# A fused channel attention and gated MLP on one core: x's product issued in the last step of the block before, its moves two steps earlier

## The chip, the cores and the metric

The kernel runs on one core of a Trainium2 chip. The metric is the device time of one execution, in microseconds (us). Each kernel is timed in several runs and the median counts; one more execution is recorded by the hardware profiler, and all rows below come from that one.

The engines are called PE (matrix products), PEld (its weight loads), DVE (vector), ACT (scalar and activation), POOL (GpSimd) and SP (here it only issues transfers). Each engine works through its own queue in program order; engines wait for each other by semaphores. A name such as L582 is line 582 of the kernel before.

## The reference

Two batches of q, k and v, each 6016 x 256, float32. In each batch the columns of q and k are normalised over the 6016 rows, a 256 x 256 score matrix is formed and its softmax `a` taken; then comes x = v a, followed by RMS normalisation of each row and a gated MLP with 1536 hidden channels:

```python
qn = q / (np.linalg.norm(q, axis=1, keepdims=True) + 1e-06)
kn = k / (np.linalg.norm(k, axis=1, keepdims=True) + 1e-06)
s = kn.transpose(0, 2, 1) @ qn / tau
...
a = np.exp(s)
a /= a.sum(-1, keepdims=True) + 1e-09
x = v @ a
...
rms = np.sqrt(np.mean(x * x, axis=-1, keepdims=True) + 1e-06)
xn = x / rms * rms_g
g = xn @ w_gate
silu = g * (1.0 / (1.0 + np.exp(-g)))
val = xn @ w_val
out = silu * val @ w_out
```

## The kernel before

**Stages.** The kernel first reads q and k of batch 0 in chunks and forms the scores, the norms and the softmax. From then on it goes through 24 blocks j of 512 rows (128 x 4; blocks 11 and 23 have three tiles of 128), 12 of each batch. Each block has 12 steps f, one for 128 hidden channels. Blocks 0 and 1 use the plain product (`emit_hidden`) beside the rest of batch 1's scores and the decoding of the weights; blocks 2 to 23 use `emit_pair`, which makes gate and value of a step from seven half-size products (a Strassen-Winograd scheme).

**Precision.** All products are made of pairs: each operand is split into a high part (`vh`, `gh`, `xt0`, `w100`) and the remainder (`vl`, `gl`, `xt1`, `w101`), and three matmuls stand for one product. ACT writes the high part (a copy into a rounded type) and POOL or DVE subtracts it to get the remainder.

**One step of `emit_pair`.** PE makes 21 matmuls `p` (L582) in four groups of 3, 6, 6 and 6, each into a PSUM tile of its own. The pool of these tiles (`ps_gv`) has four, so group g of a step must wait until group g of the step before has been read. ACT copies the first group to `a` (L595), DVE adds up the rest in L601 (needs `a` and the second group), L602 and L603 (third group) and L604 (fourth group), which leaves gate and value in `z`. In the odd step of a pair ACT applies Silu (L600) and POOL multiplies (L612, twice); in the even step behind it ACT rounds the product to `gh` (L553, twice) and POOL makes `gl` (L559, twice). Three steps later PE adds the step's part of the output, 12 matmuls `po` (L662). In step 2 the output of the block before is complete: ACT copies it to `ob` (L673) and SP issues four stores (L680).

**The next block's input.** While block j runs, the input of block n = j + 1 is made, in pieces that a table `ready` hangs behind the steps of block j (the pieces of one step follow that step's `emit_pair` and `emit_out` in every engine's queue):

- `x(h)`: half h of x = v a, 12 matmuls `px` (L386) on PE from `vt`, the split v, and `a`.
- `squares_of_x(h)`: ACT squares it and sums each row (L402); POOL makes 1/rms `rr` (L411, L415).
- `xn(h)`: ACT scales x by `rr` into `xn` (L427).
- `emit_xT_move`: DVE transposes 32 x 32 squares of `xn` into `xw` (L463, twice), and SP issues 16 transfers from `xw` to `xnT` (L470), which move the squares to their places.
- `v_moves`: DVE transposes the v of the block after next into `vw` (L366, twice), then SP issues four loads for the v one further on (L335). `v_splits`: ACT and POOL split it into `vt` (L349, L350).
- `emit_xT_parts`: ACT waits for all 16 transfers and scales `xnT` by the RMS weight (L485, twice); DVE makes the four differences of the Winograd scheme (L490, then L495 twice).
- `emit_xT_round(0)`, `emit_xT_round(1)`: ACT rounds (L507) and POOL subtracts (L509), two each, into `xt`, which the p products of the next block read.

Block 1 shares this table with the later ones; block 0 has its own, `ready0`. In blocks 4 to 7 and 10 the pieces of batch 1's softmax are added in steps 6 to 8 (`inverse_norms`, `softmax_min`, `softmax_exp`, `softmax_div`).

Of the kernel before, what the change touches and what calls it, by code (L numbers as in the profile page):

```python
# [19 lines left out]
def kernel(  # L20
# [59 lines left out]
    def f32(ap):  # L80
        return ap.bitcast(F32)
# [24 lines left out]
    def decode_w(f, piece=None):  # L106
        if piece in (None, 0):
            r = wraw[f]
            x = pool["wtmp"].tile([P, WF], U32, tag="wx", name=f"wx_{f}")
            nc.vector.tensor_scalar(  # L110
                out=x, in0=r[:, :, 0], scalar1=29, scalar2=None, op0=ALU.logical_shift_right
            )
            wval[f] = x
        if piece in (None, 1):
            x = wval[f]
            high = wraw.pop(f)[:, :, 1]
            e = pool["wtmp"].tile([P, WF], F32, tag="we", name=f"we_{f}", bufs=1)
            nc.scalar.activation(out=e, in_=high.bitcast(F32), func=AF.Copy, scale=2.0 ** -112)
            nc.vector.scalar_tensor_tensor(
                out=x, in0=high, scalar=0x80000000, in1=x,  # L120
                op0=ALU.bitwise_and, op1=ALU.bitwise_or,
            )
            wval[f] = (x, e)
        if piece in (None, 2):
            x, e = wval[f]
            nc.vector.scalar_tensor_tensor(
                out=x, in0=e.bitcast(U32), scalar=3, in1=x,
                op0=ALU.logical_shift_left, op1=ALU.bitwise_or,
            )
            wval[f] = x.bitcast(F32)  # L130
# [187 lines left out]
    for b in range(B):  # L318
        t = 0
        while t < NT:  # L320
            n = min(BT, NT - t)
            blocks.append((b, t * A, n))
            t += n
    NB = len(blocks)
# [4 lines left out]
    def load_v(j, queue=nc.sync):  # L329

        b, mu0, n = blocks[j]
        t = v_p.tile([P, A * BT, KC, S], F32, tag="v", name=f"v_{j}")
        src = v[b].rearrange("(s m) (c i r) -> i s m c r", s=S, c=KC, i=A)
        for i in range(A):
            queue.dma_start(  # L335
                out=t[S * i:S * (i + 1), :A * n].rearrange("p m c r -> p (m c) r"),
                in_=src[i][:, mu0:mu0 + A * n].rearrange("s m c r -> s (m c) r"),
            )
        v_t[j] = t

    def half_tiles(j, h):
        return list(range(2 * h, min(2 * h + 2, blocks[j][2])))
# [17 lines left out]
    def move_v(j, c):  # L360

        n = blocks[j][2]
        if c == 0:
            v_w[j] = v_p.tile([P, KC, BN], F32, tag="vw", name=f"vw_{j}")
        w = v_w[j][:, c]
        nc.vector.transpose(  # L366
            out=by_tile(w, n),
            in_=v_t[j][:, :A * n, c, :].rearrange("p (a t) r -> p a t r", a=A),
        )

    def split_v(j, c, engine=nc.vector):
        n = blocks[j][2] * P
        if c == 0:
            vT[j] = [vt_p.tile([P, KC, BN], F32R, tag=f"vt{i}", name=f"vt{i}_{j}") for i in range(2)]
        split(v_w[j][:, c, :n], [x[:, c, :n] for x in vT[j]], engine)

    def emit_x(j, h):
        ah, al = a_hl[blocks[j][0]]
        vh, vl = vT[j]
        ts = half_tiles(j, h)  # L380
        psum, tag = (ps_s, "s") if j >= WINO and h else (ps_m, "m") if j else (ps_gv, "gv")
        px = psum.tile([P, 2, C], F32, tag=tag, name=f"px_{j}_{h}")
        for c in range(KC):
            for i, t in enumerate(ts):
                for m, (w, x) in enumerate(((vh, ah), (vl, ah), (vh, al))):
                    nc.tensor.matmul(  # L386
                        out=px[:, i, :], lhsT=w[:, c, t * P:(t + 1) * P], rhs=x[:, c, :],
                        start=(i == 0 and c == 0 and m == 0),
                        stop=(c == KC - 1 and m == 2),
                        skip_group_check=True,  # L390
                    )
        xps[j, h] = px

    def emit_x_squares(j, h):
        px = xps[j, h]
        ts = half_tiles(j, h)
        if h == 0:
            xnt[j] = xn_p.tile([P, BT, C], F32, tag="xn", name=f"xn_{j}")
        xn = xnt[j][:, 2 * h:2 * h + 2, :]
        ss = st_p.tile([P, 2], F32, tag="ss", name=f"ss_{j}_{h}")  # L400
        for i in range(len(ts)):
            nc.scalar.activation(  # L402
                out=xn[:, i, :], in_=px[:, i, :], func=AF.Square, scale=C ** -0.5,
                accum_out=ss[:, i:i + 1],
            )
        xps[j, h] = (px, ss)

    def emit_rr(j, h):
        px, ss = xps[j, h]
        nn = len(half_tiles(j, h))  # L410
        nc.gpsimd.tensor_scalar(  # L411
            out=ss[:, :nn], in0=ss[:, :nn], scalar1=1e-6, scalar2=None, op0=ALU.add
        )
        rr = st_p.tile([P, 2], F32, tag="rr", name=f"rr_{j}_{h}")
        nc.gpsimd.tensor_tensor(out=rr[:, :nn], in0=ss[:, :nn], in1=mhalf[:, :nn], op=ALU.pow)  # L415
        xps[j, h] = (px, rr)

    def emit_xn(j, h, share=False):
        px, rr = xps.pop((j, h))
        for i, t in enumerate(half_tiles(j, h)):  # L420
            if share and i == 0:
                nc.vector.tensor_scalar(
                    out=xnt[j][:, t, :], in0=px[:, i, :], scalar1=rr[:, i:i + 1], scalar2=None,
                    op0=ALU.mult,
                )
                continue
            nc.scalar.activation(  # L427
                out=xnt[j][:, t, :], in_=px[:, i, :], func=AF.Copy, scale=rr[:, i:i + 1]
            )
# [67 lines left out]
    def emit_xT_round(j, i):  # L497
        h = blocks[j][2] * P // 2
        slots = ((0, 1), (1, 3)) if i == 0 else ((3, 5), (5, 7))
        hi, lo = ([y[:, a:b] for a, b in slots] for y in xp[j])  # L500
        if i == 0:
            x = [moved[j][0][:, c, :2 * h].rearrange("p (i n) -> p i n", i=2) for c in range(KC)]
            src = [x[0][:, :1], x[1]]
        else:
            src = [moved[j][1][:, m:m + 2, :h] for m in (0, 2)]
        for o, x in zip(hi, src):
            nc.scalar.activation(out=o, in_=x, func=AF.Copy)  # L507
        for o, x, y in zip(lo, src, hi):
            nc.gpsimd.tensor_tensor(out=o, in0=x, in1=f32(y), op=ALU.subtract)  # L509
# [174 lines left out]
    with tc.manual_schedule():  # L684
# [40 lines left out]
        for i in range(nch):  # L725
            n = chunks[0][i][1]
# [84 lines left out]
        for f in range(NF):  # L811
            go = [lambda: None]
            if f + 3 < NF:
                go = [lambda f=f: decode_w(f + 3, 0), lambda f=f: decode_w(f + 3, 1)]
# [7 lines left out]
            n = 2 if f % 2 else 1  # L822
# [44 lines left out]
        def v_moves(n):  # L867
            if n < NB:
                move_v(n, 0)
                move_v(n, 1)  # L870
                if 2 < n + 1 < NB:
                    load_v(n + 1)

        def v_splits(n):
            if n < NB:
                for c in range(KC):
                    split_v(n, c, nc.gpsimd)

        def x(h):
            return lambda n: emit_x(n, h)  # L880

        def squares_of_x(h):
            return lambda n: (emit_x_squares(n, h), emit_rr(n, h))

        def xn(h):
            return lambda n: emit_xn(n, h)

        ready = {
            0: (x(0),),
            2: (squares_of_x(0), x(1)),  # L890
            3: (xn(0),),
            4: (squares_of_x(1), lambda n: v_moves(n + 1)),
            5: (xn(1), emit_xT_move),
            6: (lambda n: v_splits(n + 1),),
            7: (emit_xT_parts,),
            8: (lambda n: emit_xT_round(n, 0),),
            10: (lambda n: emit_xT_round(n, 1),),
        }
        ready0 = {
            1: (v_moves,),  # L900
# [10 lines left out]
        for s, (j, f) in enumerate(steps):  # L911
            if j < WINO:
                emit_hidden(j, f, weights.get((j, f), ()))
            else:
                emit_pair(j, f)
            owed.append((j, f))
            if len(owed) > (2 if j < WINO else 3):
                emit_out(*owed.pop(0))
            n = j + 1
            if n < NB:  # L920
                for go in (ready if j else ready0).get(f, ()):
                    go(n)
            for go in extra.get((j, f), []):
                go()
# [37 lines left out]
```

## Time and profile before

| | us |
|---|---|
| runs of the kernel before (three) | 1510.26, 1510.35, 1511.95 |
| median | 1510.35 |
| the profiled execution | 1509.38 |
| its span, first to last instruction | 1507.6 |
| PE busy in the span | 1356.1 |
| POOL busy | 949.9 |
| DVE busy | 931.0 |
| ACT busy | 679.7 |
| mean granted clock of PE | 0.937 of full speed |

The profiled execution took 1.8 us more than its span. Busy PE is counted from start to modelled end of pipelined matmuls. A wait is idle time of an engine just before an instruction, put down to what released that instruction last. The granted clock of a stretch is 1.00 at full speed (2.4 GHz) and 0.50 at the lower level (1.2 GHz).

### The profile page before, as it was taken

The numbers are of one execution on the slowest core, as the hardware profiler recorded it, in microseconds if no ns is written. First come the engines' busy times: TensorE is split into PE (matmuls) and PEld (weight loads), VectorE is DVE, ScalarE is ACT, GpSimd is POOL, SyncE is SP. The second block draws the span as 40 slices with busy tenths as digits, with TensorE's granted clock in tenths as the row PEclk, the third lists the DMA queues.
The fourth block names the chain that finished last, engine by engine and source line by source line (L and its number), as shares of the span: only waits on it lengthen the run. The fifth ranks groups of instructions, "written<-read, shape, count | busy, mean of one in ns | idle before, by whom it ended". The sixth has DMA issues, their size and how long they took to land.

```text
span 1507.6 us, 27090 instructions
## 1 busy us (share of the span) xinstructions
PE 1356.1 (90%) x10212; PEld 1312.5 (87%) x10212; DVE 931.0 (62%) x1417; ACT 679.7 (45%) x1331; POOL 949.9 (63%) x824
## 2 busy tenths in 40 slices
PE   7998988899898898898898898898998988988988
PEld 6877878889898898898898898898998988988988
DVE  5689567556755665665664665665566556656655
ACT  4556545444444454443443443444444444444433
POOL 3146556766766676676765767666667766766664
PEclk8999999999998899999998999999999999999999
DMA  8857210120120110110110210201201201101001
GB/s 258 293 168 210 50 28 15 29 43 15 29 43 15 30 35 10 39 30 14 39 29 15 39 25 19 43 15 29 43 15 29 42 17 29 34 9 27 21 7 24
DMA packets 147683, 71.77 MB, mean 48 GB/s; under 512 B 100704, under 2 KB 139104, under 8 KB 147552
## 3 DMA queue, kind: packets, MB, share of 16 engines
q1 hardware_dynamic: 147168, 68.99, 18.3%
q0 software_dynamic: 384, 1.05, 0.4%
q8 instruction: 81, 1.33, 0.4%
q14 instruction: 50, 0.41, 0.1%
HBM read 46.40 MB, written 12.32 MB: 39 GB/s over the span
## 4 chain that ended last, share of the span: by engine, by line
PE 56%; DVE 14%; SPq 14%; issue 5%; DMA 5%; ACT 2%; POOL 2%; DVEq 0%; ACTq 0%; POOLq 0%
PE p L582 30%; PE po L662 16%; SPq L470 14%; PE px L386 4%; PE s L174 3%; DVE z L601 3%; DMA xnT<-xw 3%; DMA raw<-in_k_dram 2%; DVE z L602 2%; DVE z L604 2%; POOL z L612 2%; DVE vw L366 1%; ACT xnT L485 1%; DVE z L603 1%; PE pg L630 1%
## 5 line engine op out<-in xcount | busy, mean ns | idle before, releaser
L582 PE MATMUL p<-xt,w 128*128 128x256 f32 (+1 forms) x3168 | 494.6, 292 | 118.4 <-ACT a L595 80.1
L582 PEld LDWEIGHTS p<-xt,w 128*128 128x128 f32 x3168 | 436.1, 198 | 127.7 <-ACT a L595 85.1
L612 POOL TENSOR_TENSOR z<-z,z 128x512 f32<-128x512 f32 (+1 forms) x262 | 326.1, 1265 | 297.2 <-DVE z L604 297.2
L559 POOL TENSOR_TENSOR gl<-z,gh 128x512 fp32r<-128x512 f32 (+1 forms) x272 | 346.5, 1294 | 122.1 <-ACT gh L553 121.3
L662 PE MATMUL po<-w,gh 128*128 128x256 f32 x2256 | 417.0, 283 | 0.2 <-ACT gh L553 0.2
L662 PEld LDWEIGHTS po<-w,gh 128*128 128x128 f32 x2256 | 354.0, 193 | 2.4 <-ACT gh L553 0.4
L601 DVE TENSOR_TENSOR z<-p,a 128x512 f32<-128x512 f32 (+1 forms) x264 | 178.8, 677 | 282.2 <-PE p L582 270.9
L582 PE MATMUL p<-xt,s 128*128 128x256 f32 (+1 forms) x2376 | 344.1, 292 | 6.5 <-POOL xt L509 3.1
L582 PEld LDWEIGHTS p<-xt,s 128*128 128x128 f32 x2376 | 317.9, 200 | 8.1 <-DVE z L601 4.0
L662 PE MATMUL po<-w,gl 128*128 128x256 f32 x1128 | 317.8, 282 | 2.6 <-POOL gl L559 2.4
L595 ACT ACTIVATE a<-p 128x256 f32<-128x256 f32 (+1 forms) x264 | 99.1, 375 | 333.8 <-PE p L582 333.5
L553 ACT ACTIVATE gh<-z 128x512 fp32r<-128x512 f32 (+1 forms) x274 | 167.9, 621 | 133.8 <-POOL z L612 120.9
L662 PEld LDWEIGHTS po<-w,gl 128*128 128x128 f32 x1128 | 215.5, 191 | 3.4 <-POOL gl L559 3.2
L602 DVE TENSOR_TENSOR z<-p,z 128x512 f32<-128x512 f32 (+1 forms) x264 | 179.4, 680 | 33.1 <-PE p L582 7.1
L604 DVE TENSOR_TENSOR z<-p,z 128x512 f32<-128x512 f32 (+1 forms) x264 | 179.4, 680 | 28.8 <-PE po L662 0.5
L600 ACT ACTIVATE z<-z 128x1024 f32<-128x1024 f32 (+1 forms) x132 | 136.4, 1034 | 63.8 <-DVE z L604 63.7
L603 DVE TENSOR_TENSOR z<-p,z 128x256 f32<-128x256 f32 (+1 forms) x264 | 110.4, 418 | 9.0
L490 DVE TENSOR_TENSOR xp<-xnT 128x512 f32<-128x512 f32 (+1 forms) x22 | 15.3, 695 | 149.2 <-ACT xnT L485 149.2
L174 PE MATMUL s<-raw 128*128 128x256 f32 x376 | 94.4, 409 | 13.4 <-DMA raw<-in_k_dram 13.3
L485 ACT ACTIVATE xnT<-xnT,g_sb 128x512 f32<-128x512 f32 (+1 forms) x44 | 28.9, 703 | 169.7 <-DMA xnT<-xw 169.7
L174 PEld LDWEIGHTS s<-raw 128*128 128x128 f32 x376 | 75.8, 206 | 28.0 <-issue 16.6
L198 DVE TENSOR_TENSOR acc<-acc,sq 128x1024 f32<-128x1024 f32 (+1 forms) x47 | 64.0, 1362 | 31.1 <-ACT sq L189 28.9
(91 smaller groups left out, 1112.4 us busy)
## 6 DMA issues: line engine op xcount, KB each, us to landing
out_dram<-ob SPq DMA_DIRECT2D x88, 128.0 KB, 2.3
raw<-in_q_dram SPq DMA_DIRECT2D x20, 512.0 KB, 6.0
raw<-in_k_dram SPq DMA_DIRECT2D x20, 512.0 KB, 6.9
v<-in_v_dram SPq DMA_DIRECT2D x80, 128.0 KB, 3.7
xnT<-xw SPq DMA_DIRECT2D x320, 32.0 KB, 1.9
wraw<-in_moe_w_gate_dram SPq DMA_DIRECT2D x12, 256.0 KB, 3.8
wraw<-in_moe_w_val_dram SPq DMA_DIRECT2D x12, 256.0 KB, 3.9
wraw<-in_moe_w_out_dram SPq DMA_DIRECT2D x12, 256.0 KB, 5.0
```

The costliest lines, as they stand in the source:

```text
L174: nc.tensor.matmul(out=s_ps[b][:, c, :], lhsT=r[:, 1, t, c * P:(c + 1) * P], rhs=r[:, 0, t, :], start=(t0 + t == 0 and c == 0), stop=(t0 + ...
L470: nc.sync.dma_start(out=x[S * i:S * (i + 1), :, a * n * S:(a + 1) * n * S], in_=w[S * a:S * (a + 1), :, i, :n, :].rearrange("p c t s -> p ...
L553: nc.scalar.activation(out=gh, in_=hh, func=AF.Copy)
L559: engine.tensor_tensor(out=gl, in0=hh, in1=f32(gh), op=ALU.subtract)
L582: nc.tensor.matmul(out=t[:, i, :h], lhsT=wm[wi], rhs=xm[xi], start=(i == 0 and q == 0), stop=(q == 2), skip_group_check=True,)
L600: nc.scalar.activation(out=zg[:, :2 * n], in_=zg[:, :2 * n], func=AF.Silu)
L601: nc.vector.tensor_tensor(out=zz[:, 0:4:3], in0=ps[1], in1=twice(a1[:, :, :h]), op=ALU.add)
L602: nc.vector.tensor_tensor(out=zz[:, 1:3], in0=ps[2], in1=twice(zz[:, 3:4]), op=ALU.add)
L603: nc.vector.tensor_tensor(out=zz[:, 3], in0=ps[2][:, 0], in1=zz[:, 2], op=ALU.add)
L604: nc.vector.tensor_tensor(out=zz[:, 1:3], in0=ps[3], in1=zz[:, 1:3], op=ALU.add)
L612: engine.tensor_tensor(out=hh, in0=hh, in1=z[:, i * n:(i + 1) * n], op=ALU.mult)
L662: nc.tensor.matmul(out=o_ps[j][t // 2][:, t % 2, :], lhsT=g[:, t * P:(t + 1) * P], rhs=wo[w][:, f, :], start=(first and t % 2 == 0 and m = ...
```

## The change

The table `ready` becomes three. Blocks 2 to 22 use the new `ready`, block 1 gets `ready1`, block 0 keeps `ready0`. In the new `ready`:

- the first half of x's product, for block j + 2, is issued in step 11 of block j (it was in step 0 of block j + 1), the second half in step 0 (was step 2);
- squares, `rr` and `xn` of both halves stand two steps earlier: steps 0 to 3 instead of 2 to 5;
- the transposes and the 16 transfers (`emit_xT_move`) stand in step 3 instead of step 5, which is ahead of `v_moves` (still in step 4) instead of behind it;
- scaling and differences (`emit_xT_parts`) stay in step 7, the rounds in steps 8 and 10.

`ready1` has the moves in step 4, `v_moves` in step 5, the scaling in step 8 and the rounds in steps 9 and 10, and issues the first half of block 3's product in step 11. No instruction is added or taken away in these pieces.

```diff
         ready = {
-            0: (x(0),),
-            2: (squares_of_x(0), x(1)),
-            3: (xn(0),),
-            4: (squares_of_x(1), lambda n: v_moves(n + 1)),
-            5: (xn(1), emit_xT_move),
+            0: (squares_of_x(0), x(1)),
+            1: (xn(0),),
+            2: (squares_of_x(1),),
+            3: (xn(1), emit_xT_move),
+            4: (lambda n: v_moves(n + 1),),
             6: (lambda n: v_splits(n + 1),),
             7: (emit_xT_parts,),
             8: (lambda n: emit_xT_round(n, 0),),
             10: (lambda n: emit_xT_round(n, 1),),
+            11: (lambda n: n + 1 < NB and emit_x(n + 1, 0),),
+        }
+        ready1 = {
+            0: (x(0),),
+            1: (squares_of_x(0),),
+            2: (x(1), xn(0)),
+            3: (squares_of_x(1),),
+            4: (xn(1), emit_xT_move),
+            5: (lambda n: v_moves(n + 1),),
+            6: (lambda n: v_splits(n + 1),),
+            8: (emit_xT_parts,),
+            9: (lambda n: emit_xT_round(n, 0),),
+            10: (lambda n: emit_xT_round(n, 1),),
+            11: (lambda n: emit_x(n + 1, 0),),
         }
...
-                for go in (ready if j else ready0).get(f, ()):
+                for go in (ready0, ready1, ready)[min(j, 2)].get(f, ()):
                     go(n)
```

SP's queue in the kernel before, over blocks 10 to 12 (a row stands for all its equal transfers):

```order
L680 DMA out_dram<-ob_7650 32x4x256 x4
L335 DMA v_7782<-in_v_dram 32x32x32 x4
L470 DMA xnT_7842<-xw_7839 32x2x96 x16
L680 DMA out_dram<-ob_8348 32x4x256 x4
L335 DMA v_8481<-in_v_dram 32x32x32 x4
L470 DMA xnT_8539<-xw_8536 32x2x128 x16
L680 DMA out_dram<-ob_9008 32x3x256 x4
```

and in the changed kernel, the same stretch:

```order
L680 DMA out_dram<-ob_7666 32x4x256 x4
L470 DMA xnT_7735<-xw_7732 32x2x96 x16
L335 DMA v_7803<-in_v_dram 32x32x32 x4
L680 DMA out_dram<-ob_8370 32x4x256 x4
L470 DMA xnT_8438<-xw_8435 32x2x128 x16
L335 DMA v_8503<-in_v_dram 32x32x32 x4
L680 DMA out_dram<-ob_9030 32x3x256 x4
```

The 16 transfers now stand directly behind the stores, and the loads of v behind them.

ACT's queue in the kernel before, from the squares of the second half in step 4 of block 17 to the scaling in step 7 (`a_17_5` is `a` of step 5):

```order
L402 ACTIVATE xn_12495,ss_1_12618<-px_1_12502 128x256 x2
L595 ACTIVATE a_17_5_12657<-p_17_5_12632 128x256
L600 ACTIVATE z_17_2_12596<-z_17_2_12596 128x1024
L427 ACTIVATE xn_12495<-px_1_12502,rr_1_12622 128x256 x2
L595 ACTIVATE a_17_6_12730<-p_17_6_12705 128x256
L553 ACTIVATE gh_4_12667<-z_17_2_12596 128x512
L553 ACTIVATE gh_5_12669<-z_17_2_12596 128x512
L349 ACTIVATE vt_19_12753<-vw_12624 128x512 x2
L595 ACTIVATE a_17_7_12784<-p_17_7_12759 128x256
L600 ACTIVATE z_17_3_12731<-z_17_3_12731 128x1024
L485 ACTIVATE xnT_12688<-xnT_12688,g_sb 128x512 x2
```

and in the changed kernel from the last `xn` in step 3 of that block to the last row ahead of the scaling:

```order
L427 ACTIVATE xn_12389<-px_1_12396,rr_1_12521 128x256 x2
L595 ACTIVATE a_17_4_12623<-p_17_4_12598 128x256
L553 ACTIVATE gh_2_12558<-z_17_1_12488 128x512
L553 ACTIVATE gh_3_12560<-z_17_1_12488 128x512
L595 ACTIVATE a_17_5_12679<-p_17_5_12654 128x256
L600 ACTIVATE z_17_2_12624<-z_17_2_12624 128x1024
L595 ACTIVATE a_17_6_12730<-p_17_6_12705 128x256
L553 ACTIVATE gh_4_12689<-z_17_2_12624 128x512
L553 ACTIVATE gh_5_12691<-z_17_2_12624 128x512
L349 ACTIVATE vt_19_12753<-vw_12646 128x512 x2
L595 ACTIVATE a_17_7_12784<-p_17_7_12759 128x256
L600 ACTIVATE z_17_3_12731<-z_17_3_12731 128x1024
```

Between the last `xn` and the scaling there are now four steps of ACT's work where there were two.

## Rows read from the trace of the kernel before

**Rows 1.** The page's busy times of the engines: us, share, instructions.

```profile
PE 1356.1 (90%) x10212; PEld 1312.5 (87%) x10212; DVE 931.0 (62%) x1417; ACT 679.7 (45%) x1331; POOL 949.9 (63%) x824
```

**Rows 2.** Waits of the span: engine line <- releaser: us in total, times, longest.

```profile
ACT xnT L485 <- DMA xnT<-xw: 169.7, 22, 8.9
...
PE p L582 <- ACT a L595: 80.1, 24, 6.3
...
PE p L582 <- DVE z L601: 40.9, 20, 2.5
...
PE p L582 <- POOL xt L509: 3.1, 1, 3.1
```

**Rows 3.** Timeline, block 15: start us, us, engine, line, operation [idle before <- releaser].

```profile
1019.62 1.29 DVE L463 STREAM_TRANSPOSE xw<-xn 128x512 f32<-128x512 f32 x2
...
1021.05 11.32 SPq L470 DMA_DIRECT2D xnT<-xw  x16
...
1024.27 1.04 ACT L600 ACTIVATE z<-z 128x1024 f32<-128x1024 f32 x1
...
1027.32 0.88 PE L582 MATMUL p<-xt,w 128*128 128x256 f32 x6
...
1027.64 2.52 POOL L612 TENSOR_TENSOR z<-z,z 128x512 f32<-128x512 f32 x2 [0.25 <-DVE z L604]
...
1033.90 1.33 ACT L485 ACTIVATE xnT<-xnT,g_sb 128x512 f32<-128x512 f32 x2 [8.59 <-DMA xnT<-xw]
...
1035.99 1.84 DVE L495 TENSOR_TENSOR xp<-xnT,xp 128x256 f32<-128x256 f32 x2
1036.10 2.86 POOL L559 TENSOR_TENSOR gl<-z,gh 128x512 fp32r<-128x512 f32 x2 [5.93 <-ACT gh L553]
...
1037.75 0.68 DVE L601 TENSOR_TENSOR z<-p,a 128x512 f32<-128x512 f32 x1
...
1038.48 1.01 PE L582 MATMUL p<-xt,w 128*128 128x256 f32 x3 [2.06 <-DVE z L601]
...
1039.79 0.69 DVE L604 TENSOR_TENSOR z<-p,z 128x512 f32<-128x512 f32 x1
```

**Rows 4.** Chain that ended last, blocks 14 and 15: start us, us, what.

```profile
979.62 4.21 PE p L582 x18
...
992.02 1.40 PE po L662 x12
...
997.32 1.43 PE px L386 x12
...
1002.65 2.50 PE p L582 x21
```

**Rows 5.** Busy us by stretch, then granted clock, DMA share, GB/s.

```profile
1039.00:1041.00 2.00, 2.00 (x12) 2.00 (x10) 1.86 (x4) 0.49 (x1) 1.89 (x2) 0.50 0.00 0
```

**Rows 6.** First and last p product (line L582), and block 23's start in the chain.

```profile
L582 PE MATMUL p<-xt,w x3168: 250/282/583, 233.7 to 1497.4; 128*128 128x256 f32 x180, 128*128 128x192 f32 x18
...
1456.93 2.32 PE p L582 x21
```

**Rows 7.** Timeline, ACT alone, step 3 of block 15.

```profile
1008.38 0.39 ACT L595 ACTIVATE a<-p 128x256 f32<-128x256 f32 x1 [0.46 <-PE p L582]
```

**Rows 8.** Timeline, SP alone: the longest and the shortest of the 22 issue stretches.

```profile
1079.52 11.67 SPq L470 DMA_DIRECT2D xnT<-xw  x16
...
1138.00 10.18 SPq L470 DMA_DIRECT2D xnT<-xw  x16
```

**Rows 9.** Lines L490 and L495: ns of one, least/median/most, first and last start, shapes.

```profile
L490 DVE TENSOR_TENSOR xp<-xnT x22: 558/692/1019, 223.6 to 1439.6; 128x512 f32<-128x512 f32 x20, 128x384 f32<-128x384 f32 x2
...
L495 DVE TENSOR_TENSOR xp<-xnT,xp x44: 358/427/1377, 224.7 to 1440.6; 128x256 f32<-128x256 f32 x40, 128x192 f32<-128x192 f32 x4
```

**Rows 10.** Groups by line and shape on DVE, blocks 2 to 23: busy us, mean ns.

```profile
L280 DVE SCALAR_TENSOR_TENSOR z<-z,inv,iq 128x256 f32<-128x256 f32 x2 | 3.0, 1498 | 0.0
...
L303 DVE TENSOR_SCALAR a<-z,mx 128x256 fp32r<-128x256 f32 x2 | 2.1, 1050 | 0.1
```

## What was predicted before the changed kernel ran

> **What bounds the kernel now.** I read the page's busy shares first, then the waits, then one block in the chain of waits and in the timeline, and last the clock in the table by stretch. The shares [rows 1] show PE busy for 90% of the span, no other engine above 63%: PE is the bound, so what matters is where PE is not at its full pace. The waits [rows 2] say where: PE waits for ACT's copy `a` 80.1 us in all and for DVE's first sum `z` (L601) 40.9 us, each about once per block; and ACT, ahead of them, waits 169.7 us in 22 places for the transfers `xnT<-xw`. It is one event per block, and the timeline of block 15 [rows 3] shows it: DVE transposes `xn` into `xw` at 1019.62, SP issues 16 transfers from 1021.05 for 11.32 us, and ACT, which is through with its last work of step 7 at 1024.27 + 1.04 = 1025.31, sits 8.59 us until the last of them has landed. Behind ACT's scaling (L485, 1033.90) stand in ACT's queue the copy `a` of step 8, and in DVE's queue the Winograd differences (L490, L495) and then L601 of step 8, which begins at 1037.75. PE runs dry meanwhile, because the four PSUM tiles of a step are freed by just these instructions.
>
> A step at full pace is 21 products p (2.50) and 12 products po (1.40), 3.90 us; an x product (12 matmuls) is 1.43 [rows 4]. So a block should take 12 x 3.90 + 2 x 1.43 = 49.66 us. Block 15 took 1038.48 - 979.62 = 58.86 [rows 3, 4], 9.2 more: the two waits, and the 18 matmuls behind them, which took 4.21 us where 21 take 2.50. In that stretch the granted clock is 0.50 [rows 5], the lower level of 1.2 GHz, where all the steps between run at 1.00.
>
> How much is there in all? The p products begin at 233.7, and the last block begins at 1456.93 and needs 1507.6 - 1456.93 = 50.7 us to the end of the span, without a bubble [rows 6]. At full pace there lie between: 20 blocks of four tiles, 936.0; block 11 with three tiles, some 12 x (2.50 + 1.05) = 42.6 (1.05 being three quarters of 1.40); and 21 pairs of x products, 58.6 (two pairs have a half product). 936.0 + 42.6 + 58.6 + 50.7 = 1087.9, so the span would be 233.7 + 1087.9 = **1321.6** if nothing ever waited: 186 us less than the 1507.6 of the profiled run. About 5 of these belong to the head of block 2 (3.1 us of waiting for POOL's `xt` [rows 2], then slow clock), the rest, some 8.6 each, to 21 bubbles.
>
> **The change part by part.** *Products of x.* The same 12 matmuls at other places of PE's queue, 1.43 each, on the path before and after: nothing. Their inputs `vt` are split in step 6, five steps ahead of the new place. Their PSUM tile is set free in step 1 of the same block. On ACT and POOL squares, `rr` and `xn` move up two steps, with the same instructions.
>
> *Moves in step 3, scaling still in step 7.* The two transposes, 16 transfers and their wait move two steps up. When would the transposes start? In step 2 ACT has the output copies and the squares. In block 15 they end at 1008.38 - 0.46 = 1007.92 [rows 7], 5.3 after step 2 began (1002.65) [rows 4]. Today an x product follows step 2. It no longer will, so ACT is late by about 1.4 in step 3, then makes `a` (0.39), and the z chain of DVE behind it takes from 1037.75 to 1039.79 + 0.69, that is 2.73 [rows 3]. The transposes then begin some 0.7 us into step 4 (today 0.1 into step 6, which begins 7.80 before step 8 at 1027.32). From transposes to scaling is 1033.90 - 1019.62 = 14.28 with 11.32 us of issues; over the 22 blocks the issues take between 10.18 and 11.67 [rows 8], so 13.1 to 14.6. The scaling can then begin 13.8 to 15.3 after step 4 began, which is **2.1 to 3.6 us into step 7**; ACT gets there 1.9 into step 7 (1025.31, step 7 beginning 3.90 before step 8, at 1023.42). ACT's wait falls from 8 us to between 0.2 and 1.7.
>
> *Queue of SP.* The four loads of v come to stand behind the 16 issues instead of in front of them. Their data is wanted a block later, so nobody waits. The output stores stand in front as before, and were issued a step earlier. Cost nothing; if a store were late, the moves would be late with it, us for us.
>
> *What is late next.* The scaling takes 1.33, so the differences on DVE can start between 0.5 before and 1.0 after the start of step 8. L601 of step 8 has a deadline: the last tile of step 9 is reached after 15 of 21 matmuls, 1.78 into that step, and L604 of step 8 must have read it, 2.73 after L601 began. So L601 may begin 3.90 + 1.78 - 2.73 = 2.95 into step 8 at no cost. Undisturbed, L490 (0.69) and two L495 (0.43 each) [rows 9] end at 1.0 + 1.6 = 2.6 at the latest: **lower bound 0**. But L495 lasts 0.43 or 1.37 [rows 9], and the timeline shows when [rows 3]: L490 had POOL idle beside it, the second of the two L495 ran beside POOL's L559 and ended after one whole POOL operation. L490 itself shows 1.02 once. In the changed kernel these three fall on POOL's L612 pair, which begins 0.32 into step 8 and lasts 2.5 (1027.64) [rows 3]. If the two engines take turns, with some 1.2 for a POOL operation, there are two cases. DVE first: L490 ends at 0.9, L612 at 2.1, L495 at 2.4, L612 at 3.6, L495 at 3.9; L601 is 0.9 late and PE stalls 0.9. POOL first, where the transfers land late: L612 at 1.5, L490 at 2.1, L612 at 3.3, L495 at 3.6, L559 at 4.8, L495 at 5.1; PE stalls **2.2**. The upper bound is 2.2 with a slow clock behind it, another 2.1 + 0.4 as in block 15. I take half of each case without slow clock, since the stalls are split into pieces and far below the 4.16 and 2.06 that stood ahead of the drop: 1.5 x 21 = 32.
>
> The page on SBUF of the Trainium skill ("SBUF — State Buffer", section "SBUF: two separate sides") states that a DVE operation with two SBUF inputs and a GpSimd operation lock one port pair in turn, each for a whole instruction. It speaks against this change, since it puts L490 under that lock too, where the rows show it blocked once in 22; by the usual durations alone the sum below would be 32 lower.
>
> *Extra work in single blocks.* The softmax of the second batch puts DVE work into steps 6 and 7 of blocks 4, 5, 6 and 10: L280 at 1.50 in two of them, L303 at 1.05 (and a like one beside each) in block 10 [rows 10]. So far much of it lay under ACT's wait; now L601 is late by it. I take 2 us in three blocks and 3 in one, 9 together.
>
> *Sum.* 1321.6 + 32 + 9 + 2 for the head of block 2 (the x product now in front of it covers 1.4 of its 3.1 us of waiting, and much of the slow clock with it) = 1364.6 of span. Outside it the profiled run has 1509.38 - 1507.6 = 1.8, and it lies 1.0 under the median of 1510.35: **1367**.
>
> **The rivals.** *No collision* (DVE and POOL don't get into each other's way, or the slack is larger than 2.95): the 32 fall away, and the time is 1335. For it: L490 mostly ran free. Against it: 1.37 against 0.43, and the L612 pair is always there.
>
> *Collisions and the lower clock*: 21 x (2.2 + 2.5) = 99 instead of 32, 1434. For it: PE at the lower clock in every block so far. Against it: the gaps are a quarter of today's.
>
> *Slower: POOL becomes the bound.* In steps 6 to 11 POOL has six L559, six L612, two L350 and four L509: 18 operations of at most about 1.26 (half of the L612 pair) [rows 3], 22.7 us in 6 x 3.90 + 1.43 = 24.8. Its last, L509, delivers `xt` to the first step of the next block; PE waited there once, 3.1 us [rows 2]. The bubble is what lets POOL catch up today. If port waits stretched POOL's work by more than a third, it would cost over 8.6 us at each block's head, more than the bubble does; with 10 us the time is 1367 - 32 + 210 = 1545. Against it: by turns with DVE POOL loses about 1 us per block, and the x product in front of the head gives it 1.4.
>
> *It does not do what it says*: the transposes start no earlier relative to step 7, because `xn` or SP is late. Then the wait stays, 1510. The rows show nothing on the way that takes 7.8 us.
>
> **How the numbers follow.** Forecast 0.62; no collision 0.20; lower clock too 0.12; slower 0.04; no effect 0.02. A change of 0.2% is about what can be told from none. So faster 0.94, same 0.02, slower 0.04. The range goes from 1328 (no collision, and half of the extra work) to 1408, where the upper bound would hold in two blocks of three. It leaves out slower, no effect and most of the lower-clock case.
>
> **What would show it.** ACT's wait for `xnT<-xw` should fall from 169.7 to below 30 us, PE's wait for `a` to below 10. PE should keep a wait for DVE (z L601 to L604), of 1 to 2 us per block, L490's median should rise from 0.69 to above 1, and the granted clock should stay at 1.00 from step 8 to 11. The forecast is wrong if PE's waits at L582 for DVE come to under 10 us or above 60, or if it waits for `xt` at the heads of blocks.

## The result, and the profile after

The changed kernel takes **1372.57 us** (median of four runs, 1370.68 to 1375.22) against 1510.68 for the kernel before: 0.909 of its time, with a 95% interval of 0.907 to 0.910. It is 138 us faster. The prediction was 1367 with a range of 1328 to 1408.

The profiled execution took 1372.74 us with a span of 1371.0. The page's busy times and its row of the granted clock (tenths of full speed in 40 slices of the span), to be held against [rows 1]:

```profile
PE 1312.8 (96%) x10212; PEld 1271.1 (93%) x10212; DVE 955.1 (70%) x1417; ACT 678.6 (50%) x1331; POOL 960.3 (70%) x824
...
PEclk8999999999999999999999999999999999999999
```

PE's busy time fell by 43 us with the same 10212 matmuls, since fewer of them ran at the lower clock (mean granted clock 0.984, before 0.937), and its share rose from 90 to 96%. DVE became busier by 24 us with the same 1417 instructions: its differences are stretched, as shown below.

The waits of the changed kernel (us in total, times, longest), beside [rows 2]:

```profile
PE p L582 <- DVE z L601: 20.0, 14, 3.7
...
ACT xnT L485 <- DMA xnT<-xw: 9.9, 10, 2.2
...
PE p L582 <- DVE z L603: 7.8, 22, 0.4
...
PE p L582 <- POOL xt L509: 3.5, 1, 3.5
```

ACT's wait for the 16 transfers went from 169.7 to 9.9 us, and PE's wait for ACT's `a` (80.1) is no longer among them. What is left for PE is DVE's sums. Who delays those is seen in the timeline of block 15, on SP, ACT, DVE, POOL and PE, from the issue of the transfers to step 9 (start us, us, engine, line, operation):

```profile
932.81 10.25 SPq L470 DMA_DIRECT2D xnT<-xw  x16
943.15 2.60 SPq L335 DMA_DIRECT2D v<-in_v_dram  x4
...
944.65 1.33 ACT L485 ACTIVATE xnT<-xnT,g_sb 128x512 f32<-128x512 f32 x2
...
945.89 0.69 DVE L604 TENSOR_TENSOR z<-p,z 128x512 f32<-128x512 f32 x1
946.50 0.91 DVE L490 TENSOR_TENSOR xp<-xnT 128x512 f32<-128x512 f32 x1
947.44 2.83 DVE L495 TENSOR_TENSOR xp<-xnT,xp 128x256 f32<-128x256 f32 x2
950.18 0.68 DVE L601 TENSOR_TENSOR z<-p,a 128x512 f32<-128x512 f32 x1
...
946.79 3.19 POOL L612 TENSOR_TENSOR z<-z,z 128x512 f32<-128x512 f32 x2
949.94 2.71 POOL L559 TENSOR_TENSOR gl<-z,gh 128x512 fp32r<-128x512 f32 x2
...
946.38 0.88 PE L582 MATMUL p<-xt,w 128*128 128x256 f32 x6
...
952.26 0.95 PE L582 MATMUL p<-xt,s 128*128 128x256 f32 x6 [0.37 <-DVE z L603]
```

ACT now comes to the scaling with the transfers landed: no idle time stands behind its row, where [rows 3] had 8.59. Step 8 begins on PE at 946.38. The two L495, 0.43 each when alone [rows 9], take 2.83 beside POOL's L612, and L601 of step 8 begins 3.80 into the step. PE sits idle for only 0.37, later in step 9.

In block 16 POOL got in first. DVE, POOL and PE there:

```profile
997.66 1.66 DVE L490 TENSOR_TENSOR xp<-xnT 128x512 f32<-128x512 f32 x1 [0.41 <-DMA v<-in_v_dram]
999.35 2.83 DVE L495 TENSOR_TENSOR xp<-xnT,xp 128x256 f32<-128x256 f32 x2
1002.10 0.68 DVE L601 TENSOR_TENSOR z<-p,a 128x512 f32<-128x512 f32 x1
...
997.46 3.02 POOL L612 TENSOR_TENSOR z<-z,z 128x512 f32<-128x512 f32 x2
...
997.05 0.88 PE L582 MATMUL p<-xt,w 128*128 128x256 f32 x6
...
1002.84 0.62 PE L582 MATMUL p<-xt,w 128*128 128x256 f32 x3 [1.37 <-DVE z L601]
1004.18 0.95 PE L582 MATMUL p<-xt,s 128*128 128x256 f32 x6 [0.37 <-DVE z L603]
```

L490 begins 0.20 behind L612 and takes 1.66; L601 begins 5.05 into step 8, and PE sits idle for 1.37 and 0.37.

### The profile page after: what moved, and what is told of

It reads as the page before. It is cut to its first block, busy times and chain, and to the rows that moved or that the text cites. A ratio compares the mean times of both kernels' runs of the same rounds, so it can differ in the third digit from the quotient of the medians.

```text
span 1371.0 us, 27148 instructions
## 1 busy us (share of the span) xinstructions
PE 1312.8 (96%) x10212; PEld 1271.1 (93%) x10212; DVE 955.1 (70%) x1417; ACT 678.6 (50%) x1331; POOL 960.3 (70%) x824
## 4 chain that ended last, share of the span: by engine, by line
PE 59%; DVE 14%; SPq 10%; DMA 6%; issue 5%; POOL 3%; ACT 2%; DVEq 0%; POOLq 0%; ACTq 0%
PE p L582 30%; PE po L662 18%; SPq L470 10%; PE px L386 5%; DMA v<-in_v_dram 3%; PE s L174 3%; DVE xp L495 2%; DMA raw<-in_k_dram 2%; DVE z L602 2%; DVE z L601 2%; DVE xp L490 1%; POOL z L612 1%; DVE wk L536 1%; DVE z L603 1%; PE pg L630 1%
## 5 line engine op out<-in xcount | busy, mean ns | idle before, releaser
L612 POOL TENSOR_TENSOR z<-z,z 128x512 f32<-128x512 f32 (+1 forms) x262 | 338.1, 1312 | 256.6 <-DVE z L604 253.7
L582 PE MATMUL p<-xt,w 128*128 128x256 f32 (+1 forms) x3168 | 471.6, 283 | 21.2 <-DVE z L601 20.0
L582 PEld LDWEIGHTS p<-xt,w 128*128 128x128 f32 x3168 | 417.1, 190 | 25.7 <-DVE z L601 24.8
L662 PE MATMUL po<-w,gh 128*128 128x256 f32 x2256 | 411.7, 281 | 0.6 <-ACT gh L553 0.6
L601 DVE TENSOR_TENSOR z<-p,a 128x512 f32<-128x512 f32 (+1 forms) x264 | 177.4, 672 | 266.2 <-PE p L582 205.0
L559 POOL TENSOR_TENSOR gl<-z,gh 128x512 fp32r<-128x512 f32 (+1 forms) x272 | 345.9, 1294 | 15.6 <-ACT gh L553 15.2
L662 PEld LDWEIGHTS po<-w,gh 128*128 128x128 f32 x2256 | 348.1, 189 | 3.2 <-ACT gh L553 1.2
L582 PE MATMUL p<-xt,s 128*128 128x256 f32 (+1 forms) x2376 | 330.3, 282 | 11.3 <-DVE z L603 7.8
L582 PEld LDWEIGHTS p<-xt,s 128*128 128x128 f32 x2376 | 301.0, 189 | 15.5 <-PE p L582 11.5
L602 DVE TENSOR_TENSOR z<-p,z 128x512 f32<-128x512 f32 (+1 forms) x264 | 179.5, 680 | 28.9 <-PE p L582 1.1
L604 DVE TENSOR_TENSOR z<-p,z 128x512 f32<-128x512 f32 (+1 forms) x264 | 179.4, 680 | 27.6
L603 DVE TENSOR_TENSOR z<-p,z 128x256 f32<-128x256 f32 (+1 forms) x264 | 110.5, 418 | 9.0
L386 PE MATMUL px<-a,vt 128*128 128x256 f32 x564 | 76.6, 286 | 0.0
L350 POOL TENSOR_TENSOR vt<-vw,vt 128x512 fp32r<-128x512 f32 (+1 forms) x48 | 63.5, 1347 | 16.2 <-ACT vt L349 16.2
```

The lines of the kernel that those rows point to most:

```text
L386: nc.tensor.matmul(out=px[:, i, :], lhsT=w[:, c, t * P:(t + 1) * P], rhs=x[:, c, :], start=(i == 0 and c == 0 and m == 0), stop=(c == KC - ...
L559: engine.tensor_tensor(out=gl, in0=hh, in1=f32(gh), op=ALU.subtract)
L582: nc.tensor.matmul(out=t[:, i, :h], lhsT=wm[wi], rhs=xm[xi], start=(i == 0 and q == 0), stop=(q == 2), skip_group_check=True,)
L601: nc.vector.tensor_tensor(out=zz[:, 0:4:3], in0=ps[1], in1=twice(a1[:, :, :h]), op=ALU.add)
L602: nc.vector.tensor_tensor(out=zz[:, 1:3], in0=ps[2], in1=twice(zz[:, 3:4]), op=ALU.add)
L604: nc.vector.tensor_tensor(out=zz[:, 1:3], in0=ps[3], in1=zz[:, 1:3], op=ALU.add)
```

## The experiments

All times are medians, each with its ratio to the kernel before on the same chip (1508.6 us there; the change's own is to the 1510.68 above). The changed kernel is the base of the edits unless another is named. Lines may stand a few further down in an edited kernel; its L601 is then L605 or L597.

| kernel | us | ratio, 95% interval |
|---|---|---|
| moves in step 5 (e2_moves5) | 1506.6 | 0.998 to 1.000 |
| moves in step 4 (e3_moves4) | 1434.24 | 0.949 to 0.953 |
| the change: moves in step 3 | 1372.57 | 0.907 to 0.910 |
| moves in step 2 (e5_moves2) | 1355.4 | 0.897 to 0.901 |
| loads of v in step 8 (e4_vload8) | 1370.98 | 0.905 to 0.911 |
| differences spread over three steps (e1_spread) | 1330.8 | 0.880 to 0.883 |
| one input instead of two (e8_one_input) | 1330.76 | 0.879 to 0.884 |
| e1 and block 1 earlier (e7_block1) | 1329.87 | 0.878 to 0.883 |
| e1 and the softmax moved (e6_softmax) | 1326.82 | 0.877 to 0.881 |

### Where the gain comes from: the lead of the moves

Two kernels take the moves back by one and by two steps and leave the rest of the change.

```diff
-            3: (xn(1), emit_xT_move),
+            3: (xn(1),),
+            5: (emit_xT_move,),
```

> The changed kernel with the transposes and the 16 transfers back in step 5 of blocks 2 to 22; x's products, squares and xn stay in their new, earlier places. Theory (the gain is the two more steps between moves and scaling): ACT waits 8 us again in every block, and the time is that of the kernel before, 1500 to 1515. Rival (the earlier product of x brings a good part of the gain): between 1373 and 1450.

Measured: 1506.6 us, and the waits of the kernel before are back.

```profile
ACT xnT L485 <- DMA xnT<-xw: 167.9, 21, 8.6
...
PE p L582 <- ACT a L595: 80.4, 24, 5.9
...
PE p L582 <- DVE z L601: 41.2, 20, 2.6
```

All three agree with [rows 2] within 2 us. This edit also puts the loads of v ahead of the 16 transfers again, but SP issues the first transfer 1.44 us after the transposes begin with either order, so the order costs nothing. So issuing x's product earlier is worth nothing by itself; its part in the change is to have `xn` ready for the earlier moves.

```diff
-            3: (xn(1), emit_xT_move),
-            4: (lambda n: v_moves(n + 1),),
+            3: (xn(1),),
+            4: (emit_xT_move, lambda n: v_moves(n + 1)),
```

> The changed kernel with the moves in step 4, ahead of the transposes of v, so that three steps lie between moves and scaling. Theory: the scaling can begin 13.2 to 14.7 us after step 5 began, 5.4 to 6.9 into step 7; ACT waits 3.5 to 5 us, L601 of step 8 begins 5.5 to 7 into step 8 where 2.95 is free, so PE stalls 2.5 to 4 us per block instead of about 1.2, plus up to 2.5 us of slow clock: 1372.6 + 21 x (1.3 to 5) = 1400 to 1478, likeliest 1435. Rival (each step of lead is worth the same, half of the 138 us): 1441; the two differ only in the wait seen in the profile.

Measured: 1434.24 us. The waits of this kernel:

```profile
ACT xnT L485 <- DMA xnT<-xw: 61.4, 21, 4.0
...
PE p L582 <- DVE z L601: 59.7, 21, 5.2
```

One step of lead takes 72 us off, half of the whole, and the second 62. ACT's wait was 2.9 us per block where 3.5 to 5 were expected; the time still came out within 1 us of the likeliest. PE's wait of 59.7 us for L601 is 2.8 per block, inside the 2.5 to 4 expected; the rival's 1441 is 7 us off.

### What remains: the differences against POOL

The theory, from the prediction: L490 and L495 wait for whole operations of POOL, and 41 us of the time after are due to it. If so, it suffices to put the two L495 where DVE has slack, behind the sums of steps 8 and 9.

```diff
-    def emit_xT_parts(j):
+    def emit_xT_parts(j, pieces=(0, 1, 2)):
...
-        for o, i0, i1 in ((t2, b2, t1), (t4, a2, t2)):
-            nc.vector.tensor_tensor(out=o, in0=i0, in1=i1, op=ALU.subtract)
+        for k, (o, i0, i1) in enumerate(((t2, b2, t1), (t4, a2, t2))):
+            if k + 1 in pieces:
+                nc.vector.tensor_tensor(out=o, in0=i0, in1=i1, op=ALU.subtract)
...
-            7: (emit_xT_parts,),
-            8: (lambda n: emit_xT_round(n, 0),),
+            7: (lambda n: emit_xT_parts(n, (0,)),),
+            8: (lambda n: emit_xT_parts(n, (1,)), lambda n: emit_xT_round(n, 0)),
+            9: (lambda n: emit_xT_parts(n, (2,)),),
```

> The changed kernel (1372.6) with DVE's three differences spread: L490 stays in step 7, the two L495 go behind the sums of steps 8 and 9. Port theory: each difference still takes up to 1.4 us beside a POOL operation, but only one of them stands ahead of any step's L601, which then begins 2 to 2.9 us into the step, inside the 2.95 that cost nothing. PE's stall in step 9 (0.4 to 1.7 us in 21 blocks) goes, most of the softmax extras too, and the clock has no reason to drop: 1372.6 - 29 - 5 - 6 = about 1333, range 1325 to 1345. Rival (PE waits because the transfers land late, not because DVE is held up): ACT's scaling is where it was, so nothing changes, 1368 to 1376.

Measured: 1330.8 us, 41.8 less than the change alone. PE's waits for DVE in this kernel, all that are left:

```profile
PE p L586 <- DVE z L605: 1.6, 2, 1.1
...
PE p L586 <- DVE z L607: 1.3, 4, 0.4
```

This shows that the place of the differences is what costs, but not yet that POOL is the reason: fewer DVE operations in a row ahead of L601 would help too. The next kernel leaves the three operations where the change has them and takes only the second input from each: they become transposes of one operand. This kernel leaves the subtraction out; it is there for its time alone.

```diff
-        nc.vector.tensor_tensor(
-            out=t[:, 0:3:2, :h], in0=x[:, :, h:2 * h],
-            in1=x[:, 0, :2 * h].rearrange("p (i n) -> p i n", i=2), op=ALU.subtract,
-        )
-        for o, i0, i1 in ((t2, b2, t1), (t4, a2, t2)):
-            nc.vector.tensor_tensor(out=o, in0=i0, in1=i1, op=ALU.subtract)
+        for o, i0 in ((t[:, 0:3:2, :h], x[:, :, h:2 * h]), (t2, b2), (t4, a2)):
+            nc.vector.transpose(out=o, in_=i0)
```

> The changed kernel with the three differences in step 7 replaced by DVE transposes of 32 x 32 squares of one operand, in the same places, with the same outputs and element counts (the subtractions are left out). Port theory: an operation with one SBUF input isn't held up by POOL (the transposes L463 took 0.67 us beside L612 as well as alone), so the three take about 0.7 + 0.4 + 0.4, L601 of step 8 begins inside its slack and PE's stall of 0.4 to 1.7 us in step 9 goes: 1372.6 - 29 to 35 = 1335 to 1345. Rival (the place in DVE's queue costs it, whatever the operation): they take 0.9 to 1.4 each as before and the time stays at 1368 to 1376.

Measured: 1330.76 us, the same as with the differences spread. The timeline of this kernel in block 15, DVE and POOL:

```profile
917.01 1.35 DVE L491 STREAM_TRANSPOSE xp<-xnT 128x512 f32<-128x512 f32 x3
...
917.31 2.55 POOL L608 TENSOR_TENSOR z<-z,z 128x512 f32<-128x512 f32 x2
```

All three operations pass beside POOL's pair in 1.35 us. In the changed kernel they took 0.91 + 2.83 at the same place. By shape (busy us, mean ns of one), first the changed kernel, then this one:

```profile
L495 DVE TENSOR_TENSOR xp<-xnT,xp 128x256 f32<-128x256 f32 x40 | 52.4, 1310 | 1.4
```

```profile
L491 DVE STREAM_TRANSPOSE xp<-xnT 128x256 f32<-128x256 f32 x40 | 14.6, 402 | 0.0
```

1310 ns against 402 for the same shape. The kind of operation changed too, from a subtraction to a transpose. That this is not the reason is seen from DVE's sums L602 to L604: they are the same kind of operation as L495, with one operand from PSUM and one from SBUF. All 264 runs of L603 in the changed kernel (ns of one, least/median/most):

```profile
L603 DVE TENSOR_TENSOR z<-p,z x264: 357/424/426, 244.4 to 1361.1; 128x256 f32<-128x256 f32 x120, 128x192 f32<-128x192 f32 x12
```

It never takes more than 0.426, though much of it runs beside POOL (in block 15 from 951.69, beside the L559 that began at 949.94); L602 and L604 never take more than 0.694. So it is the second SBUF input beside POOL's work, not the number of operations, their kind or their place alone. The Trainium skill ("SBUF — State Buffer", section "SBUF: two separate sides") states this rule, that a DVE operation with two SBUF inputs and a GpSimd operation that reads SBUF exclude each other for a whole instruction; the rows of L495, L491 and L603 agree with it.

A third kernel gives the transfers one step more of lead, with both halves of x's product in step 11:

```diff
-            0: (squares_of_x(0), x(1)),
-            1: (xn(0),),
-            2: (squares_of_x(1),),
-            3: (xn(1), emit_xT_move),
+            0: (squares_of_x(0),),
+            1: (xn(0), squares_of_x(1)),
+            2: (xn(1), emit_xT_move),
```

> The changed kernel with both halves of x's product in step 11 of the block before and the moves in step 2, so that five steps lie between moves and scaling. Theory: the transfers always land before ACT arrives, so its wait is 0, and L490 always comes ahead of POOL's L612; the blocks in which L490 ran 1.3 to 1.7 us (about nine) lose 1.3 us of stall, the others keep theirs, since the collision of L495 with L612 and L559 stays: 1372.6 - 9 x 1.3 = 1361, range 1355 to 1369. Rival (late transfers are all of the stall): 1372.6 - 30 = 1343.

Measured: 1355.4 us. ACT's wait for the transfers is gone from the list. Lines L490 and L495 of this kernel (ns of one, least/median/most):

```profile
L490 DVE TENSOR_TENSOR xp<-xnT x22: 548/682/912, 220.7 to 1284.5; 128x512 f32<-128x512 f32 x20, 128x384 f32<-128x384 f32 x2
...
L495 DVE TENSOR_TENSOR xp<-xnT,xp x44: 424/1395/1407, 221.5 to 1286.5; 128x256 f32<-128x256 f32 x40, 128x192 f32<-128x192 f32 x4
```

L490 now always comes ahead of POOL's L612 (at most 0.91), while L495 still collides in nearly every block (median 1.395): the transfers no longer matter, the collisions do. The rival's 1343 is not reached. The time is 5.6 below the likeliest. From the first scaling to the last this kernel is 14.8 us shorter than the change (1065.7 against 1080.4), where 11.7 were expected. Its first p product of block 2 also begins earlier, at 230.06 instead of 233.40, but this is no gain of the edit: in e2 and e3, which have the change's code up to that place, it begins at 230.84 and 229.43, so executions differ by that much.

### Is L490 held by a load of v?

In the changed kernel the trace names the loads `v<-in_v_dram` as what L490 waits for (2.7 us in five places), and the chain that ended last runs through them. They now stand directly behind the 16 transfers on SP. A kernel was to issue them in step 8 instead:

```diff
-            4: (lambda n: v_moves(n + 1),),
+            4: (lambda n: v_moves(n + 1, False),),
...
-            8: (lambda n: emit_xT_round(n, 0),),
+            8: (lambda n: emit_xT_round(n, 0), lambda n: 4 <= n + 1 < NB - 1 and load_v(n + 2)),
```

> The changed kernel with the four loads of v issued in step 8 of blocks 2 to 22 instead of right behind the 16 moves. The trace of the changed kernel names the loads of v as what released L490 in several blocks. Theory (they only land at that moment, and L490 waits for DVE's own L604 or for ACT's scaling): the time stays, 1368 to 1377. Rival (the loads hold up L490 or the last moves): L490 and the scaling come up to 0.5 us earlier and 5 to 12 us are saved, 1360 to 1367.

Measured: 1370.98 us (1367.89 to 1372.19), within the spread of the change alone, and a wait is still put down to those loads (3.7 us, three places). But the edit moves nothing. SP has no other instruction between steps 4 and 8, so the loads keep their place in its queue; in block 15 SP issues them at 942.82, where the changed kernel has 943.15:

```profile
942.82 2.57 SPq L335 DMA_DIRECT2D v<-in_v_dram  x4
```

So this run decides neither for the theory nor for the rival. The trace of the changed kernel does. In all five places L490 begins 0.02 to 0.04 us behind the end of ACT's scaling. In block 16 it begins at 997.66, and the scaling ends at 996.29 + 1.34 = 997.63:

```profile
996.29 1.34 ACT L485 ACTIVATE xnT<-xnT,g_sb 128x512 f32<-128x512 f32 x2 [0.87 <-DMA xnT<-xw]
```

L490 waits for the scaling, and the trace named the wrong releaser. Block 21, in which no loads are issued, shows the same wait (0.65, put down to ACT there), and its transfers are no faster: 14.46 us from the transposes to the scaling.

### The rest: the softmax and the head of block 2

On top of e1, the pieces of batch 1's softmax move to steps with slack on DVE:

```diff
-        at(4, 6, lambda: inverse_norms(1))
+        at(4, 1, lambda: inverse_norms(1))
...
-        at(5, 7, lambda: softmax_min(1, 0))
-        at(6, 7, lambda: softmax_min(1, 1))
+        at(5, 5, lambda: softmax_min(1, 0))
+        at(6, 5, lambda: softmax_min(1, 1))
...
-        at(B1 - 2, 6, lambda: softmax_div(1, 0))
-        at(B1 - 2, 7, lambda: softmax_div(1, 1))
+        at(B1 - 2, 1, lambda: softmax_div(1, 0))
+        at(B1 - 2, 5, lambda: softmax_div(1, 1))
```

> The kernel with spread differences (1330.8) with batch 1's softmax pieces moved out of steps 6 and 7 of blocks 4, 5, 6 and 10 into steps 1 and 5, where DVE and POOL have less. Theory: what is left of PE's waits for L601 in those blocks (3 us and some slow clock) goes, 1324 to 1329. Rival (the pieces cost as much wherever they stand): 1329 to 1333.

Measured: 1326.82 us (1325.9 to 1328.18), 4.0 below e1 and the lowest of all. The intervals of the two ratios overlap, but the traces bear the 4.0 out: from the first scaling to the last this kernel takes 1036.3 us and e1 1040.4, and the stretches with the softmax (named below) are some 4.5 shorter. PE's longest wait left in blocks 2 to 23 is that of 3.5 us for POOL's `xt` at the head of block 2. The last kernel goes for that one, again on top of e1:

```diff
-            8: (emit_xT_parts,),
-            9: (lambda n: emit_xT_round(n, 0),),
-            10: (lambda n: emit_xT_round(n, 1),),
+            7: (emit_xT_parts,),
+            8: (lambda n: emit_xT_round(n, 0),),
+            9: (lambda n: emit_xT_round(n, 1),),
```

> The kernel with spread differences (1330.8) with block 1's scaling back in step 7 and its two rounds in steps 8 and 9 instead of 9 and 10, so that POOL makes the last of block 2's input ahead of the two weight sums of step 10. Theory (the 3.5 us wait at the head of block 2 is L509 standing behind these sums in POOL's queue): the wait for L509 goes, and with it some of the slow clock, 1324 to 1329. Rival (the sums, now later by the two L509, make ACT's first copy of block 2 late by as much): 1330 to 1336.

Measured: 1329.87 us (1324.12 to 1332.63), which can't be told from e1 and lies between the theory's range and the rival's. The wait for `xt` is gone, and this one is new:

```profile
PE p L586 <- DVE z L648: 4.0, 1, 4.0
```

POOL's work on the weights (L531, the L527 of the change) now runs behind the rounds, at 234.69, and the chain of waits goes from there over DVE's operations on the same weights (L540) to L648 and to PE: 4.0 us of waiting in the place of 3.5. This is the rival's mechanism.

## Why the prediction was right

**The bound, and what the moves take away.** Right, by the waits after and by e2 and e3. The transfers took as long as assumed: in the eleven blocks in which ACT sat idle before the scaling, 13.8 to 14.6 us from the transposes to it (13.1 to 14.6 predicted). That idle time came to at most 2.2 us, and to none in the other eleven blocks (0.2 to 1.7 predicted for each).

**The floor.** 1321.6 was some 4 us too high. The first half product of block 3 lies ahead of 233.4 in the changed kernel and is no longer part of the sum (1.4); for the three-tile block 11 the sum took 2.50 per step for the p products, where the row of block 23 in [rows 6] has 2.32 (12 x 0.18 = 2.2); and the p products begin 0.3 earlier. That makes 1317.7.

**The head of block 2.** Mis-sized. The term was 2 us, on the reasoning that the x product now in front of it would cover part of POOL's lateness. PE at that place in the changed kernel:

```profile
233.40 0.88 PE L582 MATMUL p<-xt,w 128*128 128x256 f32 x6
...
237.93 2.22 PE L582 MATMUL p<-xt,s 128*128 128x256 f32 x8 [3.53 <-POOL xt L509]
...
242.13 2.76 PE L386 MATMUL px<-a,vt 128*128 128x256 f32 x12
244.69 0.92 PE L582 MATMUL p<-xt,w 128*128 128x256 f32 x6
```

From 233.40 to 244.69 are 11.3 us for 21 p and one x product, 3.93 at full pace: 7.4 lost, part of it at the lower clock (0.50 granted from 238 to 244). POOL reaches L509 only at 236.43, behind two operations on the weights (L527) that begin at 232.74 and one L559: its time is set by its own queue, so starting PE's x product earlier covered nothing.

**The collisions.** Right in mechanism and, but for the clock, in size. L601 was forecast 0.9 late with DVE first and 2.2 with POOL first; block 15 has 3.80 - 2.95 = 0.85 and block 16 has 5.05 - 2.95 = 2.1. How much they cost in all is read from the scalings (L485 on ACT), one per block. First the changed kernel, blocks 1, 3, 7, 10, 11 and 22 of the 22; then e1, the same blocks:

```profile
221.47 1.32 ACT L485 ACTIVATE xnT<-xnT,g_sb 128x512 f32<-128x512 f32 x2
...
322.02 1.34 ACT L485 ACTIVATE xnT<-xnT,g_sb 128x512 f32<-128x512 f32 x2 [0.89 <-DMA xnT<-xw]
...
535.93 1.34 ACT L485 ACTIVATE xnT<-xnT,g_sb 128x512 f32<-128x512 f32 x2 [1.25 <-DMA xnT<-xw]
...
686.92 1.11 ACT L485 ACTIVATE xnT<-xnT,g_sb 128x384 f32<-128x384 f32 x2
742.79 1.34 ACT L485 ACTIVATE xnT<-xnT,g_sb 128x512 f32<-128x512 f32 x2 [2.23 <-DMA xnT<-xw]
...
1301.88 1.11 ACT L485 ACTIVATE xnT<-xnT,g_sb 128x384 f32<-128x384 f32 x2
```

```profile
221.06 1.32 ACT L486 ACTIVATE xnT<-xnT,g_sb 128x512 f32<-128x512 f32 x2
...
320.59 1.34 ACT L486 ACTIVATE xnT<-xnT,g_sb 128x512 f32<-128x512 f32 x2 [0.99 <-DMA xnT<-xw]
...
522.28 1.33 ACT L486 ACTIVATE xnT<-xnT,g_sb 128x512 f32<-128x512 f32 x2 [0.97 <-DMA xnT<-xw]
...
670.21 1.13 ACT L486 ACTIVATE xnT<-xnT,g_sb 128x384 f32<-128x384 f32 x2 [0.33 <-DMA xnT<-xw]
721.34 1.34 ACT L486 ACTIVATE xnT<-xnT,g_sb 128x512 f32<-128x512 f32 x2 [2.11 <-DMA xnT<-xw]
...
1261.41 1.11 ACT L486 ACTIVATE xnT<-xnT,g_sb 128x384 f32<-128x384 f32 x2
```

From the first to the last the change takes 1080.41, e1 1040.35: 40.1 more. The stretches with the softmax (block 3 to 7, and 10 to 11) take 213.9 + 55.9 in the change and 201.7 + 51.1 in e1: 17.0 of the 40.1. The other 16 blocks have 23.1, which is 1.44 each; the forecast was 1.5.

**The softmax and the lower clock.** Those five blocks (3 to 6 and 10) were given 5 x 1.5 + 9 = 16.5; they cost 17.0 and the 4.0 that stay in e1 until e6 moves the pieces, 21. The forecast put the lower clock at nothing, and this is the term that it missed: PE ran at 0.50 for a stretch in each of blocks 3, 6, 10 and 11, three of them among these five. One minus the granted clock, added up over each stretch, gives some 1.7 us for each, an estimate; e1 has none in these blocks. Without it the five blocks come to 21 - 5.1 = 16, and the other 16 to 21.4, 1.34 each, both a little under the forecast. The forecast's reason, that the stalls would be far below those ahead of the drop (4.16 and 2.06), did not hold: in block 3 it came behind one of 1.36.

**Sum.** 1317.7 + 7.4 + 23 + 21 = 1369.1 against a span of 1371.0; 2 us are not assigned. Predicted were 1364.6. So the hit within 6 us rests on errors that partly cancel: the head of block 2 (+5.4) and the bubbles (44 for 41, with 6.8 of lower clock that had been put at nothing), against the floor (-3.9). The range's ends, 1328 and 1408, are by the prediction's own terms spans, so that as times they should have been about 3 us higher; the measured time is far inside either way.

**What was to show it.** ACT's wait for the transfers below 30: 9.9. PE's for `a` below 10: none. PE's for DVE between 10 and 60 in all: 27.8. L490's median above 1 us: no, 0.905, since in most blocks DVE came first and waited only for the rest of POOL's operation before; the mean of the full shape is 1.085. Granted clock 1.00 in steps 8 to 11: in 17 of 21 blocks.

**The rivals.** No collision (1335): not what happened, and e8, which makes it so, measures 1331. The lower clock everywhere (1434): behind a collision it fell in four blocks only. POOL as the bound: PE waits for `xt` at one head, that of block 2, as before, although POOL is busy for 70%; e6 has it at 72% and no further such wait. No effect: e2 is what that would have been.

## What to carry to other kernels

A long transfer on the way to the next block is hidden by the distance between its issue and its first use; moving its producer earlier is worth something only if the transfer moves too. When such a wait goes, cost the work that was running inside it at the durations it will have at its new place: here DVE operations with two SBUF inputs, which beside POOL's took 1.31 us instead of 0.43. Such operations go where POOL's next operation is not yet ready (L490 in e5, 0.68 in the median), or one at a time into DVE's gaps (e1). A form that reads one SBUF operand, where the computation has one, would do as well: that is what e8 shows of the time.

## What had not been expected

**The clock fell after some short gaps and not after longer ones.** Three stretches of two us of the changed kernel (the granted clock is the column before the last two):

```profile
698.00:700.00 2.00, 1.62 (x9) 1.45 (x9) 1.83 (x4) 0.60 (x1) 0.13 (x1) 0.68 0.00 0
700.00:702.00 2.00, 2.00 (x11) 2.00 (x11) 1.48 (x3) 0.46 (x1) 0.00 (x0) 0.50 0.00 0
...
1002.00:1004.00 2.00, 0.97 (x6) 0.77 (x6) 1.86 (x4) 0.23 (x1) 2.00 (x3) 1.00 0.00 0
```

Behind PE's wait of 3.74 us that ended at 697.37 the clock went to the lower level, 0.50, until about 702. In block 16, with 1.37 and 0.37 of waiting, it stayed at 1.00. But it also fell behind a wait of 1.36 us in block 3 (ended at 328.54) and stayed up behind one of 1.98 us in block 5 (436.00), so the length of the gap alone does not tell. What does was not tried.

**One short wait became a constant.** A PE wait for L603, 0.37 or 0.38 us long in nearly all of them, stands in 22 places of the changed kernel (7.8 us in all) and in four of e1 (1.3): it goes with the collision ahead of it, not with L603.
